# Loading v of four more blocks as fp16 on GpSimd's queue, and turning q and k of four more blocks by DMA, in a fused sliding-window attention and MLP kernel

## The chip, the cores and the metric

The kernel runs on one core of one Trainium2 chip. The metric is the device time of one execution in microseconds. Before the change the median of 8 runs is 321.86 us (321.04 to 322.49).

## What is computed

q, k and v are fp32 tensors of 8 batches, 8 heads, 576 positions and 64 values per head. Attention looks back over a window of 128 positions and carries a bias that falls with distance. Its output, 4608 rows of 512, goes through a layer norm with a gain and a two-layer MLP with a residual. Cut to what matters:

```
scores = scale * q @ k.T
scores = where((rel >= 0) & (rel < 128), scores - slope_h * abs(rel), -1e9)
x  = softmax(scores) @ v                     # all heads side by side: 4608 x 512
xn = (x - mean) / sqrt(var + 1e-6) * g_ln
out = x + relu(xn @ w_ch1) @ w_ch2           # 512 x 2048 and 2048 x 512
```

## The kernel before, in words

The 4608 rows are cut into 36 blocks of 128. One pair of batches has nine blocks (`PERIOD`), and the fifth of these holds the end of one batch and the start of the next, so its loads come in two halves.

**Attention, block by block** (`attention(i)`, L527). q and k are loaded, made fp16, and turned so that the head dimension lies on the partitions (`qkt`). The scores of a block against itself and the block before it go to PSUM (L687), with the bias added by a matmul with a distance table in blocks 0 to 4 (L703) and multiplied in afterwards as a mask table from block 5 on (L742). ScalarE takes the exponential (L735). TensorE multiplies with `vx`, v in fp16 with a column of ones (L759), and VectorE divides (L776, L780), takes the statistics (L797, L802) and makes `xs` (L808). `xs` is turned into `xt`, by TensorE for blocks 0 to 11 (L820) and by DMA from 12 on (L835).

**MLP, chunk by chunk** (`mlp(c)`, L857). Blocks are gathered in chunks of 3, 2, 3 and then 4. For each of 16 slices of the hidden layer four matmuls (L869) go to a PSUM bank, and ScalarE or VectorE takes the ReLU (L881, L879). Then, for each block, four groups of four matmuls (L897) follow, VectorE adds the residual (L905), and SP stores the block (L913). Below, a *weight group* is four such matmuls. The weights are loaded as fp16 by GpSimd's queue in eight pieces of 512 KB (L518, L520), four of each matrix.

**How q, k and v come in.** There are three ways.
- *Spans* (`SPANS`, L453): blocks 0 and 1, 2 and 3, 5 and 6, 7 and 8 load q and k of two blocks in one 512 KB DMA on SP's queue. An engine casts it (L594, L596), TensorE turns it in 4 fp32 transposes (L603).
- *Plain loads* (L358): q and k of block 4, and v of blocks 0 to 8, come as fp32 on SP's queue, and GpSimd or ScalarE casts them (L540, L542, L573, L575).
- *Cast loads* (`load_cast`, L461 and L466): from block 9 on (`LOAD_CAST`), q, k and v come as fp16 by a casting DMA on GpSimd's queue.

The fp16 q and k of blocks 4 and 9 to 12 are turned by TensorE in 8 transposes (L649) and evicted from PSUM (L657, L659); from block 13 on (`QK_BY_DMA`) they are turned by a DMA on SP's queue (L664).

**What sets the order.** All work is given to a planner (`Plan`, L47) as tasks with costs, dependencies, priorities and due times. It plays the queues and engines through and writes down the order in which every engine's instructions stand; each engine then runs its own list in that order. The tables `PICK` (which engines may take a cast or an eviction), `PRI`, `HOLD` and `SLACK` steer it. `LANDING` holds the latencies that it assumes for DMAs. `TABLE_AFTER` and `MIX_AFTER` name the block after whose product with v the mask tables may be made (L431, L439). Up to block `SPLIT` the scores are made in two halves. Up to 26 us of planned time (`WARM`), planned gaps of TensorE are filled with warm-up matmuls (L932).

`W_AFTER` says behind which step each weight piece is issued: a third of the number is a block, the rest says q, k or v of it. All cast loads wait for the last piece:

```
W_AFTER = [9, 10, 11, 12, 20, 23, 26, 28]
t_w[n] = plan.transfer(f"w{n}", "POOL", 0.8, 3.2, 0.0, emit, [casts[at % 3]] + last, av(i, -60.0))
for t in cast_loads:
    t.deps.append(t_w[7][0])
```

In a span, each of the three stands for the cast of v. So the first three pieces follow the cast of v of block 3.

Of the kernel before, what the change touches and what calls it, by code (L numbers as in the profile page):

```python
# [10 lines left out]
FP16 = mybir.dt.float16  # L11
# [35 lines left out]
class Plan:  # L47
# [8 lines left out]
    LANDING = {"DMA SP": (0.7, 1.3), "DMA ACT": (0.7, 1.3), "DMA POOL": (1.6, 1.4)}  # L56
# [170 lines left out]
def kernel(  # L227
# [15 lines left out]
    P = 128  # L243
# [26 lines left out]
    TABLE_AFTER = 2  # L270
    MIX_AFTER = 3
    SPLIT = 4
    LOAD_CAST = 9
    HALVED = []
    SPANS = [0, 2, 5, 7]
    SLACK = (0.1, 0.2, 0)
    PICK = {('xt', 0): 'ACT DVE', ('xt', 8): 'ACT', ('cv', 5): 'POOL', ('cv', 0): 'ACT', ('ev', 8): 'DVE', ('ev', 1): 'DVE', ('ev', 3): 'ACT', ('ck', 8): 'ACT', ('cq', 5): 'POOL', ('ev', 5): 'ACT', ('ck', 2): 'POOL', ('ck', 7): 'ACT', ('cq', 6): 'POOL', ('cq', 2): 'ACT', ('xt', 6): 'ACT DVE', ('cq', 8): 'POOL', ('xt', 5): 'DVE', ('cv', 7): 'POOL ACT', ('cv', 3): 'POOL', ('xt', 3): 'DVE', ('ev00', 4): 'DVE ACT', ('cs1', 1): 'POOL', ('cs0', 0): 'POOL', ('ev10', 3): 'ACT', ('xt', 2): 'ACT DVE', ('cq', 3): 'POOL', ('cs0', 8): 'POOL', ('ev01', 8): 'DVE ACT', ('ev10', 8): 'DVE ACT', ('ev11', 5): 'ACT', ('cs0', 2): 'ACT', ('cq', 4): 'POOL ACT', ('ev00', 8): 'DVE ACT', ('ev01', 0): 'DVE', ('cv', 8): 'POOL', ('ev11', 0): 'ACT', ('cv', 4): 'POOL ACT', ('ev01', 6): 'DVE', ('cv', 6): 'ACT', ('ev10', 5): 'ACT', ('cs1', 4): 'POOL ACT', ('ev', 0): 'DVE ACT', ('cv', 2): 'POOL', ('ev00', 2): 'DVE ACT', ('ev00', 7): 'ACT', ('ev10', 2): 'ACT', ('xt', 1): 'ACT', ('ev11', 8): 'ACT', ('xt', 4): 'DVE', ('ev00', 1): 'DVE', ('cv', 1): 'ACT', ('ev01', 7): 'DVE ACT', ('ev11', 6): 'DVE ACT', ('cq', 1): 'POOL ACT', ('ev01', 4): 'DVE ACT', ('cs0', 5): 'ACT', ('ev', 7): 'DVE ACT', ('xt', 7): 'ACT', ('ev', 9): 'ACT', ('cv', 9): 'POOL', ('cq', 11): 'POOL', ('cs1', 9): 'POOL ACT', ('ev00', 10): 'ACT', ('eva', 5): 'DVE', ('cka', 9): 'POOL DVE ACT', ('cv', 11): 'ACT', ('cqa', 10): 'POOL', ('ckb', 10): 'POOL', ('ck', 10): 'ACT', ('ev00', 5): 'DVE ACT', ('ckb', 3): 'POOL ACT', ('evb', 5): 'DVE ACT', ('ev', 11): 'DVE ACT', ('ev01', 2): 'DVE ACT', ('ckb', 6): 'ACT', ('eva', 11): 'ACT', ('cqb', 7): 'POOL', ('cka', 1): 'ACT', ('ev00', 3): 'DVE ACT', ('cq', 0): 'POOL', ('ev01', 5): 'ACT', ('cqb', 5): 'DVE', ('ev10', 4): 'DVE ACT', ('ev01', 9): 'DVE', ('cqa', 8): 'POOL DVE ACT', ('ev10', 10): 'DVE ACT', ('evb', 4): 'ACT', ('cqb', 8): 'POOL DVE ACT', ('cs0', 9): 'POOL', ('cka', 3): 'DVE', ('cqa', 2): 'DVE', ('cka', 8): 'ACT', ('cqa', 5): 'DVE', ('cq', 7): 'ACT', ('ck', 1): 'POOL ACT', ('cka', 0): 'ACT', ('cqa', 7): 'POOL', ('ev10', 11): 'ACT', ('cqa', 4): 'POOL DVE ACT', ('ev11', 11): 'ACT', ('eva', 10): 'ACT', ('ev11', 4): 'DVE', ('eva', 3): 'ACT', ('ev11', 2): 'DVE ACT', ('cqa', 6): 'DVE', ('cqa', 9): 'DVE', ('cqa', 11): 'POOL', ('ev', 2): 'DVE ACT', ('cs0', 4): 'POOL DVE', ('ckb', 11): 'POOL ACT', ('ckb', 2): 'POOL', ('ck', 5): 'POOL', ('cs1', 8): 'ACT', ('ev01', 10): 'DVE ACT', ('ev', 10): 'ACT', ('cq', 10): 'ACT', ('eva', 4): 'DVE ACT', ('cv', 10): 'ACT', ('ev', 6): 'DVE ACT', ('ck', 11): 'ACT', ('cs1', 11): 'POOL ACT', ('cqb', 1): 'DVE', ('ckb', 7): 'DVE', ('ev11', 1): 'ACT', ('ck', 4): 'ACT', ('cka', 11): 'DVE', ('ckb', 0): 'ACT', ('cs1', 0): 'POOL DVE', ('eva', 7): 'DVE ACT', ('cs0', 11): 'POOL ACT', ('evb', 8): 'DVE ACT', ('ev10', 6): 'DVE', ('eva', 2): 'DVE', ('cqb', 2): 'POOL DVE ACT', ('cq', 9): 'POOL ACT', ('ev10', 9): 'DVE', ('ev10', 0): 'DVE', ('evb', 6): 'DVE', ('eva', 8): 'ACT', ('cqa', 3): 'DVE', ('ck', 9): 'POOL ACT', ('evb', 3): 'DVE', ('cs0', 1): 'POOL', ('cqb', 9): 'ACT', ('cqb', 0): 'DVE', ('evb', 2): 'DVE ACT', ('evb', 1): 'DVE ACT', ('cqb', 6): 'ACT', ('eva', 9): 'DVE ACT', ('evb', 10): 'ACT', ('cqb', 11): 'DVE', ('cka', 10): 'POOL ACT', ('ck', 6): 'POOL', ('ckb', 1): 'POOL', ('ev10', 7): 'DVE ACT', ('cs1', 7): 'POOL', ('ev01', 3): 'DVE ACT', ('cs0', 7): 'POOL', ('cs0', 6): 'POOL ACT', ('cs1', 3): 'ACT', ('cka', 2): 'POOL', ('cqa', 1): 'ACT', ('ev01', 1): 'DVE ACT', ('cs0', 10): 'POOL ACT', ('cka', 4): 'POOL ACT', ('ev00', 6): 'ACT', ('xt', 10): 'ACT DVE'}
    PRI = {'mnewc': 2.9, 'Sa2': 1.9, 'nm0.4': 4.0, 'eT5.01': 6.2, 'pva1': -8.8, 'exb1': -4.1, 'xt0': -3.9, 'r0.14': -4.9, 'ks7.i': 6.9}
    HOLD = {'w5.i': 45.07, 'T7.1': 46.04, 'exb6': 45.43, 'r1.2': 36.4, 'eT2.01': 14.22, 'bn7': 65.04, 'r0.5': 30.1, 'bn0': 12.95, 'v1.i': 2.75, 'r1.4': 36.86, 'rc0.3': 22.89, 'rs1': 31.48}
    BY_BIAS = 5  # L280
    MASK_AT = 5
    QK_BY_DMA = 13
# [8 lines left out]
    def ring(name, n, shape, dt):  # L291
        return plan.ring([sb(f"{name}{i}", shape, dt) for i in range(n)])
# [16 lines left out]
    v32 = ring("v32", 5, [P, H, D], FP32)  # L309
    qk16 = ring("qk16", 6, [P, 2, d_model], FP16)  # L310
    vx = ring("vx", 7, [P, H, VD], FP16)
# [94 lines left out]
    d_row = plan.transfer("g", "ACT", 0.5, 0.02, 0.0, lambda e, b: nc.scalar.dma_start(out=g_row[:, :], in_=moe_g_ln.unsqueeze(0)), (), -8e5)[1]  # L406
# [42 lines left out]
    def load_span(name, src, r, n, i, v):  # L449
        (_, _, b, s0), = where(i)  # L450

        def emit(e, bank):
            nc.sync.dma_start(  # L453
                out=r[n][:, :, :],
                in_=src[b, :, s0 : s0 + 2 * P, :].rearrange("h (p t) d -> p h (t d)", t=2),
            )
        t, d = plan.transfer(f"{name}{i}", "SP", 0.6, 1.75, 1.0, emit, (), v)
        r.writes(n, t)
        return d

    def load_cast(name, src, i, dst, v):  # L461

        got = []
        for p0, n, b, s0 in where(i):
            def emit(e, bank, p0=p0, n=n, b=b, s0=s0):
                nc.gpsimd.dma_start(out=dst(p0, n), in_=src[b, :, s0 : s0 + n, :].rearrange("h p d -> p h d"))  # L466
            got.append(plan.transfer(f"{name}{i}", "POOL", 1.0 if n == P else 0.9, 1.24 if n == P else 0.76, 0.0, emit, (), v))
        return [t for t, d in got], [d for t, d in got]

# [3 lines left out]
    cast_loads = []  # L473
    for i in range(NBLK):
        nrm[i] = len([1 for j in range(i) if j not in span_of])
    for i in range(NBLK):
        vl = av(i) - 300
        if i in span_of:
            n = span_of[i]
            if SPANS[n] == i:  # L480
                span_load[n] = (load_span("qs", q, qs, n, i, vl), load_span("ks", k, ks, n, i, vl + 0.01))
            loads[i] = (None, None, load("v", v, v32, i, vl + 0.02))
            continue
        if i in HALVED:
            part = [slice(0, H // 2), slice(H // 2, H)]
            qk = [[load("qk"[a] + "ab"[x], (q, k)[a], (q32, k32)[a], i, vl + 0.004 * x + 0.002 * a, nrm[i], part[x]) for x in range(2)] for a in range(2)]
            loads[i] = (qk[0], qk[1], load("v", v, v32, i, vl + 0.02))
            continue
        if i >= LOAD_CAST:
            m = nrm[i]  # L490
            tq, dq_ = load_cast("q", q, i, lambda p0, n, m=m: qk16[m][p0 : p0 + n, 0, :].rearrange("p (h d) -> p h d", d=D), vl)
            tk, dk_ = load_cast("k", k, i, lambda p0, n, m=m: qk16[m][p0 : p0 + n, 1, :].rearrange("p (h d) -> p h d", d=D), vl + 0.01)
            tv, dv_ = load_cast("v", v, i, lambda p0, n, i=i: vx[i][p0 : p0 + n, :, 0:D], vl + 0.02)
            cast_loads += tq + tk + tv
            for t in tq + tk:
                qk16.writes(m, t)
            for t in tv:
                vx.writes(i, t)
            loads[i] = (dq_, dk_, dv_)
            continue  # L500
        loads[i] = (
            load("q", q, q32, i, vl, nrm[i]),
            load("k", k, k32, i, vl + 0.01, nrm[i]),
            load("v", v, v32, i, vl + 0.02),
        )

    W_AFTER = [9, 10, 11, 12, 20, 23, 26, 28]
# [19 lines left out]
    def attention(i):  # L527
# [48 lines left out]
        if i < LOAD_CAST:  # L576
            cv = [add(f"cv{i}", pick("cv", "POOL", POOL=0.64, ACT=0.62), e_cv, lv_, av(i, 0.2))]
            v32.reads(i, cv[0]); vx.writes(i, cv[0])
            weights(i, (cv[0],) * 3 if i in span_of else (cq[-1], ck[-1], cv[0]))
        else:  # L580
            weights(i, (None, None, None))
# [341 lines left out]
    for t in cast_loads:  # L923
        t.deps.append(t_w[7][0])
# [48 lines left out]
```

## Time and profile before

| what | before |
|---|---|
| median of 8 runs | 321.86 us |
| the profiled execution's own time | 322.49 us |
| its span, first to last instruction | 320.8 us |
| TensorE busy | 313.2 us (98%) |
| VectorE, ScalarE, GpSimd busy | 182.8, 166.1, 95.0 us |
| transposes of fp16 q and k on TensorE (L649) | 40 |
| warm-up matmuls (L932) | 102 |
| DMA transposes of q and k (L664), time to landing | 23, 3.0 to 9.1 us |
| granted TensorE clock | 1.00 |

How to read the page: PE is the matmul row of TensorE, PEld its weight loads, DVE is VectorE, ACT ScalarE, POOL GpSimd, SP the sync engine that issues DMAs. Times are in microseconds from the first instruction. In a timeline a line gives start, duration, engine, source line, operation, output<-inputs and the number of instructions; in brackets stands the idle time before it and what ended it. The slices show the busy tenths in 40 equal parts of the span. In the table of stretches each line has the stretch, its length, and then busy time and number of instructions of PE, PEld, DVE, ACT and POOL, the clock, the busy share of the DMA engines and GB/s. A matmul's shown duration is longer than the distance to the next one, since they are pipelined; costs are therefore read from start to start.

### The profile page before, as it was taken

What the parts mean: (1) busy time and instruction counts of PE and PEld (TensorE: products, weight loads), DVE (VectorE), ACT (ScalarE), POOL (GpSimd) and SP (SyncE); (2) the same over time, 40 slices, a digit from 0 to 9 for tenths busy, and PEclk for the clock granted to TensorE, in tenths of its full rate; (3) what the DMA queues carried; (4) which work ended last, traced back from release to release, by engine and by line L of the source; (5) the groups of instructions that cost most, each with busy time, mean ns of one, the idle gap of its engine ahead of it and who ended that gap; (6) DMA issues with size and microseconds to landing.
All of it is one profiled execution on the core that took longest, in us unless ns stands there. A gap on an engine that the chain in (4) does not pass through costs nothing.

```text
span 320.8 us, 6445 instructions
## 1 busy us (share of the span) xinstructions
PE 313.2 (98%) x2584; PEld 170.9 (53%) x2584; DVE 182.8 (57%) x408; ACT 166.1 (52%) x269; POOL 95.0 (30%) x124
## 2 busy tenths in 40 slices
PE   8998999999999999999999999999999999999995
PEld 6875675466645554444454445444444454444453
DVE  3597387299745856755665566546655665221012
ACT  2987885059705852475257525752575257305600
POOL 4250349468631816803372531201100000000000
PEclk9999999999999999999999999999999999999999
DMA  8999988999999999999999999727700220011011
GB/s 192 233 203 211 222 160 123 172 230 166 155 142 199 140 108 112 172 173 143 173 170 177 86 165 182 80 51 131 133 16 18 82 85 16 19 66 65 2 65 65
DMA packets 151120, 40.93 MB, mean 128 GB/s; under 512 B 134065, under 2 KB 146609, under 8 KB 151090
## 3 DMA queue, kind: packets, MB, share of 16 engines
q0 software_dynamic: 88608, 14.82, 64.6%
q1 hardware_dynamic: 62480, 25.70, 38.5%
q8 instruction: 20, 0.33, 0.4%
q14 instruction: 10, 0.08, 0.1%
q10 hardware_dynamic: 2, 0.00, 0.0%
HBM read 36.70 MB, written 9.44 MB: 144 GB/s over the span
## 4 chain that ended last, share of the span: by engine, by line
PE 87%; DMA 5%; DVE 3%; SPq 3%; issue 0%; POOL 0%
PE fb L897 39%; PE fb L869 37%; PE sc L687 5%; PE fb L759 4%; DMA w1sb<-in_moe_w_ch_dram 3%; DMA v<-in_v_dram 2%; SPq L358 1%; SPq L453 1%; DVE xs L808 1%; PE fb L820 1%; PE fb L649 1%; PE fb L603 1%; DVE ot L905 0%; DVE st L797 0%; DVE xb L780 0%
## 5 line engine op out<-in xcount | busy, mean ns | idle before, releaser
L869 PE MATMUL fb<-xt,w1sb 128*128 128x512 f16 (+2 forms) x640 | 133.6, 358 | 1.5 <-DMA w1sb<-in_moe_w_ch_dram 1.4
L897 PE MATMUL fb<-w2sb,ht 128*128 128x512 f16 (+1 forms) x592 | 134.2, 373 | 0.0
L881 ACT ACTIVATE ht<-fb 128x512 f16<-128x512 f32 (+2 forms) x144 | 80.4, 562 | 81.0 <-PE fb L869 79.2
L869 PEld LDWEIGHTS <-w1sb 128*128 128x128 f16 x640 | 59.9, 98 | 56.9 <-DMA w1sb<-in_moe_w_ch_dram 1.9
L735 ACT ACTIVATE probs<-sc 128x1024 f16<-128x1024 f32 (+1 forms) x72 | 67.2, 974 | 35.5 <-PE sc L687 35.5
L897 PEld LDWEIGHTS <-ht 128*128 128x128 f16 x592 | 54.7, 98 | 57.8
L905 DVE SCALAR_TENSOR_TENSOR ot<-fb,rstd,xb 128x512 f32<-128x512 f32 (+1 forms) x37 | 27.3, 737 | 62.6 <-PE fb L897 62.0
L466 POOL DMA_DIRECT2D vx<-in_v_dram x30 | 25.4, 847 | 92.1 <-PE fb L759 89.0
L742 DVE TENSOR_TENSOR probs<-probs,mreg 128x1024 f16<-128x1024 f16 (+1 forms) x48 | 30.5, 653 | 23.1 <-ACT probs L735 22.8
L780 DVE TENSOR_TENSOR xb<-fb,rec 128x256 f16<-128x256 f32 x72 | 30.2, 422 | 2.1
L759 PEld LDWEIGHTS <-probs 128*128 128x128 f16 x544 | 24.7, 97 | 11.4
L808 DVE SCALAR_TENSOR_TENSOR xs<-xb,mv,g_t 128x512 f16<-128x512 f16 x36 | 28.4, 790 | 1.0
L466 POOL DMA_DIRECT2D qk<-in_q_dram x30 | 25.9, 867 | 5.8 <-DMA w2sb<-in_moe_w_ch_dram 2.6
L759 PE MATMUL fb<-vx,probs 128*128 128x65 f16 x544 | 26.9, 193 | 0.0
L466 POOL DMA_DIRECT2D qk<-in_k_dram x30 | 26.0, 873 | 2.2 <-DMA w2sb<-in_moe_w_ch_dram 1.7
L797 DVE BATCH_NORM_STATS2 st<-xb 128x6 f32<-128x512 f16 x36 | 24.9, 693 | 1.0
L776 DVE RECIPROCAL rec<-fb 128x4 f32<-128x4 f32 x72 | 12.5, 177 | 19.0 <-PE fb L759 18.9
L687 PEld LDWEIGHTS <-qkt 64*128 64x128 f16 x544 | 15.3, 94 | 11.9 <-issue 11.1
L687 PE MATMUL sc<-qkt 64*128 64x128 f16 x288 | 19.4, 216 | 0.0
L687 PE MATMUL sc<-qkt,qkt 64*128 64x128 f16 x256 | 18.2, 219 | 0.0
L879 DVE TENSOR_SCALAR ht<-fb 128x256 f16<-128x256 f32 (+2 forms) x16 | 8.7, 548 | 8.1 <-PE fb L869 7.6
L596 POOL CAST ks<-ks 128x1024 f16<-128x1024 f32 x3 | 4.0, 1331 | 22.1 <-DMA ks<-in_k_dram 22.1
(61 smaller groups left out, 122.4 us busy)
## 6 DMA issues: line engine op xcount, KB each, us to landing
out_dram<-ot SPq DMA_DIRECT2D x35, 256.0 KB, 2.8
qk<-in_q_dram POOLq DMA_DIRECT2D x24, 128.0 KB, 7.2
qk<-in_k_dram POOLq DMA_DIRECT2D x24, 128.0 KB, 7.2
vx<-in_v_dram POOLq DMA_DIRECT2D x24, 128.0 KB, 5.2
qs<-in_q_dram SPq DMA_DIRECT2D x4, 512.0 KB, 7.9
ks<-in_k_dram SPq DMA_DIRECT2D x4, 512.0 KB, 7.6
v<-in_v_dram SPq DMA_DIRECT2D x8, 256.0 KB, 6.3
w1sb<-in_moe_w_ch_dram POOLq DMA_DIRECT2D x4, 512.0 KB, 11.2
```

The costliest lines, as they stand in the source:

```text
L466: nc.gpsimd.dma_start(out=dst(p0, n), in_=src[b, :, s0 : s0 + n, :].rearrange("h p d -> p h d"))
L687: nc.tensor.matmul(scs[half][:, g, c0 : c0 + P], kt[rows, 1, hp, :], qkt[i][rows, 0, hp, :], start=not bias, stop=True, skip_group_check=True,
L735: nc.scalar.activation(out=o, in_=n_, func=AF.Exp, scale=inv_sqrt_d)
L742: en.tensor_tensor(out=pv, in0=pv, in1=mask[:, 2 * half : 2 * half + 2, :, lo:], op=ALU.mult)
L759: nc.tensor.matmul(pp[:, hh * (D + 1) : hh * (D + 1) + D + 1], probs[i][:, bank, slot, side * P : side * P + P], vx[i - 1 + side][:, h, 0 ...
L780: nc.vector.tensor_tensor(out=xb[i][:, 256 * half : 256 * half + 256].rearrange("p (h d) -> p h d", d=D), in0=pp[:, :, 0:D], in1=rec[2 * i ...
L797: nc.vector.bn_stats(out=st[i][:, :], in_=xb[i][:, :])
L808: nc.vector.scalar_tensor_tensor(out=xs[i][:, :], in0=xb[i][:, :], scalar=mv[c][:, j, 0:1], in1=g_t[:, :], op0=ALU.subtract, op1=ALU.mult,)
L869: nc.tensor.matmul(fb[b][:, 0:n_], w1sb[:, kb, f * P : f * P + P], xt[c][:, kb, 0:n_], start=(kb == 0), stop=(kb == NKB - 1),)
L881: nc.scalar.activation(out=ht[c][:, f, 0:n_], in_=src, func=AF.Relu)
L897: nc.tensor.matmul(pm[:, 0 : c1 - c0], ht[c][:, f, j * P : j * P + P], w2sb[:, f, c0:c1], start=(f == 0), stop=(f == NFB - 1),)
L905: nc.vector.scalar_tensor_tensor(out=ot[i][:, c0:c1], in0=fb[plan.held[key][1]][:, 0 : c1 - c0], scalar=rstd[c][:, j : j + 1], in1=xb[i][: ...
```

## The change

v of blocks 5 to 8 (`V_CAST`) is loaded by the casting DMA straight into `vx`, so that the fp32 loads and casts of these four blocks go. `W_AFTER` changes: the first weight piece follows the cast of v of block 2, the next two that of block 3, the fourth the load of v of block 5, the fifth and sixth that of block 7, the last two the load of k of block 9. The cast loads no longer wait for the last weight piece; they are chained in order of block, each behind the load before it and the pieces that stand ahead of it. `QK_BY_DMA` falls from 13 to 8; as 7 and 8 are a span, q and k of blocks 9 to 12 are now turned by DMA. The mask tables are allowed one block later, block 4's scores are made in two halves, some costs that the planner assumes change, and `PICK`, `PRI`, `HOLD` and `SLACK` are new.

The instructions counted in both programs: plain v loads on SP fall from 10 to 6, cast loads of v on GpSimd rise from 30 to 34, casts of v fall from 9 to 5, transposes of fp16 q and k on TensorE from 40 to 8, their 128x1024 evictions from 5 to 1, DMA transposes of q and k rise from 23 to 27, warm-up matmuls fall from 102 to 97. On SP's queue v of block 1 now stands ahead of q of blocks 2 and 3. GpSimd's list of DMAs begins: weight piece 0, 1, 2, v of 5, piece 3, v of 6, v of 7, pieces 4 and 5, the cast of q of 7 and 8, v of 8, q and k of 9, the cast of k of 7 and 8, pieces 6 and 7. Between pieces 0 and 1 stand the casts of v of 3 and q of 4, between pieces 2 and v of 5 the cast of v of 4. On TensorE the first half of block 4's product with v now stands ahead of the first MLP matmul, and the q turn of blocks 5 and 6 stands eight weight groups after that point instead of six.

```diff
-    LANDING = {"DMA SP": (0.7, 1.3), "DMA ACT": (0.7, 1.3), "DMA POOL": (1.6, 1.4)}
+    LANDING = {"DMA SP": (0.7, 1.3), "DMA ACT": (0.7, 1.3), "DMA POOL": (2.1, 1.4)}
...
-    TABLE_AFTER = 2
-    MIX_AFTER = 3
-    SPLIT = 4
+    TABLE_AFTER = 3
+    MIX_AFTER = 4
+    SPLIT = 5
     LOAD_CAST = 9
+    V_CAST = 5
...
-    SLACK = (0.1, 0.2, 0)
+    SLACK = (0, 0.3, 0)
...
-    QK_BY_DMA = 13
+    QK_BY_DMA = 8
...
+    def load_v(i, v):
+        if i < V_CAST:
+            return load("v", v_in, v32, i, v)
+        tv, dv_ = load_cast("v", v_in, i, lambda p0, n: vx[i][p0 : p0 + n, :, 0:D], v)
+        cast_seq.append((3 * i + 2, tv))
+        for t in tv:
+            vx.writes(i, t)
+        return dv_
...
-    W_AFTER = [9, 10, 11, 12, 20, 23, 26, 28]
+    W_AFTER = [7, 10, 10, 17, 22, 22, 28, 28]
...
+        seq = dict(cast_seq)
+        third = seq[3 * i + 2][-1] if i >= V_CAST else cv[0]
+        if i in span_of:
+            weights(i, (third,) * 3)
+        elif i >= LOAD_CAST:
+            weights(i, (seq[3 * i][-1], seq[3 * i + 1][-1], third))
+        else:
+            weights(i, (cq[-1], ck[-1], third))
...
-    for t in cast_loads:
-        t.deps.append(t_w[7][0])
+    cast_seq.sort(key=lambda x: x[0])
+    for n, (at, tasks) in enumerate(cast_seq):
+        before = [t_w[m][0] for m, w_at in enumerate(W_AFTER) if (w_at // 3 * 3 + 2 if w_at // 3 in span_of else w_at) < at][-1:] + (cast_seq[n - 1][1] if n and at < 27 else [])
+        for t in tasks:
+            t.deps += before
```

## The prediction

> **What bounds the kernel now.** I read the page's busy row and slices first, then the busy time by stretches, then the first 45 us of TensorE and GpSimd in order of time, then the chain that ended last, and at the end the DMA issues.
>
> The page says where the limit is:
>
> ```profile
> PE 313.2 (98%) x2584; PEld 170.9 (53%) x2584; DVE 182.8 (57%) x408; ACT 166.1 (52%) x269; POOL 95.0 (30%) x124
> PE   8998999999999999999999999999999999999995
> PEclk9999999999999999999999999999999999999999
> ```
>
> TensorE is the bound and its clock is full throughout, so only work taken off it, or waits and fillers, can move the end. By stretches:
>
> ```profile
> 20.00:26.00 6.00, 4.24 (x77) 3.50 (x76) 4.98 (x14) 6.00 (x14) 2.03 (x3) 1.00 1.16 213
> 42.00:50.00 8.00, 7.56 (x96) 6.32 (x94) 7.55 (x18) 5.79 (x12) 4.13 (x6) 1.00 0.65 113
> 90.00:120.00 30.00, 30.00 (x240) 14.96 (x239) 18.28 (x38) 16.41 (x25) 11.51 (x14) 1.00 1.71 151
> ```
>
> The second figure is TensorE. From 90 us it never idles. What can be won or lost is the work itself and the first 90 us: 1.76 us idle at 20 to 26, 0.44 at 42 to 50, and the warm-up matmuls that fill the rest before 26. TensorE in order of time:
>
> ```profile
> 20.37 0.62 PE L649 MATMUL fb<-iden,qk 128*128 128x128 f16 x8
> 20.82 0.41 PE L759 MATMUL fb<-vx,probs 128*128 128x65 f16 x8
> ...
> 24.07 0.45 PE L932 MATMUL fb<-warm_t 128*128 128x128 f16 x5
> 25.93 1.47 PE L869 MATMUL fb<-xt,w1sb 128*128 128x384 f16 x8 [1.41 <-DMA w1sb<-in_moe_w_ch_dram]
> 27.24 0.41 PE L759 MATMUL fb<-vx,probs 128*128 128x65 f16 x8
> ...
> 30.88 0.60 PE L603 MATMUL fb<-iden,qs 128*128 128x128 f32 x4
> ```
>
> The first MLP matmul waits 1.41 us for the first weight piece. The chain says why that piece is late, and GpSimd's row shows the order in which it is issued:
>
> ```profile
> 9.68 7.25 DMA v<-in_v_dram
> 16.93 0.05 issue
> 16.98 0.56 POOL vx L575
> 17.54 8.35 DMA w1sb<-in_moe_w_ch_dram
> ```
> ```profile
> 14.32 0.62 POOL L575 CAST vx<-v 128x512 f16<-128x512 f32 x1
> 16.98 0.62 POOL L575 CAST vx<-v 128x512 f16<-128x512 f32 x1 [2.05 <-DMA v<-in_v_dram]
> 17.54 0.92 POOL L518 DMA_DIRECT2D w1sb<-in_moe_w_ch_dram  x1
> ```
>
> The piece is issued behind the cast of v of block 3, whose load lands at 16.93, and lands at 25.89.
>
> **Transposes of blocks 9 to 12 (QK_BY_DMA).** Only four blocks move, since 7 and 8 are a span. Each loses 8 transposes; in the rows above the next instruction starts 0.45 us after them (20.37 to 20.82), as at 68.03, 72.86 and 81.94. 4 x 0.45 = **-1.8 us**, straight off the bound. Four evictions of 128x1024 go too (0.67 us on VectorE, 1.02 on ScalarE), off the path. Four DMA transposes come onto SP's queue, between stores; the 23 existing ones land 3.0 to 9.1 us after issue. In the new order the q and k of block 9 are issued ahead of the last two weight pieces, and its scores stand 20 us of TensorE work after the first use of the second matrix, those of 10 to 12 later still, so I take 0. If that cover were gone, each late block would cost at most its 9.1 us less the weight work queued ahead of it.
>
> **First weight piece.** W_AFTER puts it behind the cast of v of block 2, which ran at 14.32 to 14.88, so it is issued at 14.88: 2.66 earlier. The same 8.35 makes it land at 23.2. That piece alone would free the start: the last turn of chunk 0 (xt, VectorE at 23.62 for 0.42) ends at 24.04, so the first MLP matmul could run at 24.1 and not 25.93, **-1.8**. The instruction counts fit: 97 warm-up matmuls for 102.
>
> **What the earlier piece collides with.** Packets of the two queues, counted from the trace (KB per us):
>
> ```
> 17.5-19.0  SP alone, 256-byte packets    about 190
> 19.5-20.5  SP alone, 512-byte packets    about 240
> 21.5-28    GpSimd's 1 KB packets 140, SP's 512-byte packets  72
> 31-34      GpSimd's 1 KB packets 146, SP's 256-byte packets  36
> ```
>
> GpSimd's first packet left at 20.37, 2.83 us after its issue, when the 256-byte loads up to v of block 4 had finished (19.3). Moved by 2.66 it leaves at 17.7 and is near full flow at 18.3, with some 170 KB of v of block 4 outstanding: 170/36 = 4.7 us, so 23.1 instead of 19.3. A completion took 1.1 us (data at 19.3, landing at 20.39): landing 24.2, cast 0.6, and its first product with the probabilities, which in the new order stands *ahead of* the first MLP matmul, is at 24.8 and takes 0.25. First MLP matmul about 25.1, 0.8 earlier than now.
>
> The next is q of blocks 5 and 6 (512 KB, landed 26.83 before). It now starts at 23.1: 512/72 = 7.1, plus 1.1, lands at 31.3; ScalarE's cast takes 1.36, so its turn on TensorE can run at 32.7 and not 30.88. TensorE gets there at 25.1 + 8 weight groups x 0.667 + 0.55 = 31.0 and waits 1.7 us. It has done two groups more than before by then (1.33), so it is 32.7 - 30.88 - 1.33 = **+0.5 us behind**, the 0.8 spent. k of the same span then lands by 38.4 (7.1 later), is cast by 40, and is wanted at 32.7 + 7.7 = 40.4: 0.
>
> A rule of the Trainium skill would make this worse: DMA: Bandwidth & Descriptors, under Specifications, gives GpSimd's path a first byte after about 1 us. With it the packets would start at 15.9, with most of k and v of block 4 (over 400 KB) still to come: 11 us at 36 KB/us, and the first MLP matmul near 29. The row says 2.83 (and 2.7 at the second weight matrix); I take the row.
>
> **v of blocks 5 to 8.** Four 256 KB fp32 loads and their four casts (GpSimd 0.61, 1.05, 0.62; ScalarE 0.63) go; four 128 KB cast loads come, each 0.9 us of GpSimd. The same page and section says that rows under 512 bytes fall below line rate, against halving v's rows to 128 bytes. In the trace cast loads queued without company land 0.95 us apart (61.69, 62.67, 63.61, 64.55), an fp32 load 1.29 after the one before it (12.97, 14.26). By the rule each would be dearer than what it replaces, some 2 us in all before the second matrix; by the row cheaper. I take the row: 0, and the casts were off the path. What they do is clear SP's queue: the second q/k span no longer stands behind v of block 5 (landing 38.61).
>
> **Second weight matrix, and what waits on GpSimd.** Its first two pieces no longer sit behind casts (issued 38.31 and 47.82 before); they follow the queue of 512 KB at 3.65 us each and land some 4 us earlier. But the last two stand behind GpSimd's casts of q and k of blocks 7 and 8, so a late span delays them and the cast loads between. Cost between -0.4 (the 0.41 us that TensorE waits near 48 for VectorE's xs of block 5 vanishes) and +2.5 (below); the nearest row is that 0.41, met by an order that is no longer there: -0.4.
>
> **Masks, split of block 4, picks.** Mask tables move behind block 4's first exponentials (8 x 0.3 us on ScalarE, which is full at 20 to 26), which lets the product of block 4 stand ahead of the first MLP matmul. If they delay the first ReLUs: three PSUM banks give about 2 us of cover; beyond it up to 0.5. I take 0. The new engine choices move evictions between engines at 52 and 57%: 0, bounds -0.3 and +0.3.
>
> **Sum.** -1.8 + 0.5 - 0.4 = -1.7 on the profiled 322.49 (span 320.80 and 1.69 around it), giving 320.8. That execution is 0.63 above the median of 321.86; on the median 320.2.
>
> **Rivals.**
> *No collision.* SP's loads keep pace (loads of one queue overlap, so less is outstanding than I count). Then -1.8 (turns), -1.8 (start), -0.25 (product already done), -0.4: **317.6**. For it: the first idle is 1.41 us and goes in full. Against: the 36 KB/us row.
> *Slower: SP starved behind GpSimd.* The place is the q of blocks 7 and 8. If q of 5 and 6 needs another 0.8 us, and three spans flow at 72 KB/us without relief, q of 7 lands at 32.1 + 2 x 7.1 = 46.3 at worst, about 45 with part of the queue empty; cast 1.33 on GpSimd: the turn runs at 46.4 for 43.38 now, with 0.2 us more done: +2.8, and the last weight pieces follow. -1.8 + 2.8 = +1.0, less part of 0.4: **322.6**. It decides when the loss before 50 us passes 2.2. Against: the small v packets between weights leave SP more.
> *The turns give nothing.* A DMA transpose of 9 to 12 is late, or TensorE waits as long as it saved: **321.8**.
>
> **How the numbers follow.** Forecast 0.40 (319.0 to 321.3), no collision 0.25 (317.2 to 318.8), starved 0.23 (322.4 to 323.5), nothing 0.12. A measurement of this kernel tells about 0.2%, 0.64 us, from no change. Faster 0.60 (forecast nearly whole, no collision), same 0.16, slower 0.24. The range takes the forecast, most of no collision and the nearer half of starved: 317.5 to 322.9.
>
> **What would show it.** Right: 8 instead of 40 transposes of qk on TensorE; the first piece issued near 14.9 and landed near 23.2; the first MLP matmul at 25.1, released by v of block 4; a wait of 1 to 2 us at the q turn of blocks 5 and 6 near 32.7; no idle after 90. Wrong: that turn before 31 (no collision), or idle over 1 us at the turns of 7 or at the last pieces of the second matrix (starved); a first piece that still lands at 25 would break the step that everything in the start rests on.

## The result and the profile after

The changed kernel takes 319.69 us in the median of 12 executions (319.01 to 321.83), the kernel before 321.98 (33 executions on the same chip, 321.04 to 325.42 and one of 462.0); the ratio is 0.9932 with a 95% interval of 0.9914 to 0.9949. The profiled executions stand at 320.42 (span 318.7) and 322.49 (span 320.8): 2.07 us. Executions of one kernel differ by some us (by 2.8 for the changed kernel), in part through a collision that the experiments bring out, so a run's range is given with its median.

The busy row of the page after:

```profile
PE 311.3 (98%) x2547; PEld 169.2 (53%) x2547; DVE 180.7 (57%) x411; ACT 164.3 (52%) x261; POOL 96.9 (30%) x125
```

TensorE is still the bound, with 1.9 us less to do. The stretches (after the length: TensorE, its weight loads, VectorE, ScalarE, GpSimd, then clock, DMA share, GB/s):

```profile
20.00:26.00 6.00, 6.00 (x100) 4.80 (x98) 5.71 (x17) 5.43 (x10) 3.30 (x4) 1.00 1.21 237
26.00:34.00 8.00, 7.34 (x56) 4.59 (x55) 6.48 (x16) 7.16 (x18) 3.00 (x4) 1.00 1.30 216
34.00:42.00 8.00, 6.65 (x51) 4.79 (x50) 1.87 (x5) 5.16 (x10) 4.83 (x5) 1.00 1.45 204
42.00:50.00 8.00, 8.00 (x104) 6.15 (x102) 6.69 (x17) 5.41 (x8) 5.79 (x8) 1.00 1.62 191
```

The idle time at 20 to 26 and at 42 to 50 is gone; a new one of 1.35 us stands at 34 to 42, and 0.66 at 26 to 34 (0.18 before). TensorE in order of time shows where:

```profile
24.61 0.42 PE L773 MATMUL fb<-vx,probs 128*128 128x65 f16 x8
24.86 1.46 PE L883 MATMUL fb<-xt,w1sb 128*128 128x384 f16 x8
...
28.70 2.77 PE L883 MATMUL fb<-xt,w1sb 128*128 128x384 f16 x16 [0.29 <-DVE mnew L440]
31.31 0.60 PE L617 MATMUL fb<-iden,qs 128*128 128x128 f32 x4
31.75 0.39 PE L834 MATMUL fb<-iden,xs 128*128 128x128 f16 x4
32.43 5.39 PE L883 MATMUL fb<-xt,w1sb 128*128 128x384 f16 x40 [0.29 <-DMA w1sb<-in_moe_w_ch_dram]
39.17 1.47 PE L883 MATMUL fb<-xt,w1sb 128*128 128x384 f16 x8 [1.35 <-DMA w1sb<-in_moe_w_ch_dram]
```

The first MLP matmul runs at 24.86 (25.93 before) and waits for nothing; the q turn of blocks 5 and 6 (L617) waits for nothing either. The longest wait is now for the fourth weight piece. The chain that ended last, and GpSimd in order of time, say the same:

```profile
24.64 14.48 DMA w1sb<-in_moe_w_ch_dram
39.12 0.05 issue
39.17 1.47 PE fb L883 x8
```
```profile
14.27 1.05 POOL L582 CAST vx<-v 128x512 f16<-128x512 f32 x1
15.27 0.92 POOL L525 DMA_DIRECT2D w1sb<-in_moe_w_ch_dram  x1
...
17.94 0.62 POOL L549 CAST qk<-q 128x512 f16<-128x512 f32 x1 [1.13 <-DMA q<-in_q_dram]
18.50 1.48 POOL L525 DMA_DIRECT2D w1sb<-in_moe_w_ch_dram  x2
...
23.76 0.89 POOL L467 DMA_DIRECT2D vx<-in_v_dram  x1
24.64 0.76 POOL L525 DMA_DIRECT2D w1sb<-in_moe_w_ch_dram  x1
```

The first piece is issued at 15.27 and lands at 21.52. The fourth stands behind v of block 5: issued at 24.64, landed at 39.12.

### The profile page after: what moved, and what is told of

It reads as the page before. It is cut to its first block, busy times and chain, and to the rows that moved or that the text cites. A ratio compares the mean times of both kernels' runs of the same rounds, so it can differ in the third digit from the quotient of the medians.

```text
span 318.7 us, 6377 instructions
## 1 busy us (share of the span) xinstructions
PE 311.3 (98%) x2547; PEld 169.2 (53%) x2547; DVE 180.7 (57%) x411; ACT 164.3 (52%) x261; POOL 96.9 (30%) x125
## 4 chain that ended last, share of the span: by engine, by line
PE 92%; DMA 5%; DVE 1%; ACT 1%; issue 0%
PE fb L911 40%; PE fb L883 36%; PE sc L701 6%; PE fb L773 5%; DMA w1sb<-in_moe_w_ch_dram 5%; PE fb L949 2%; PE sc L717 1%; PE fb L617 1%; PE fb L834 1%; PE fb L410 1%; ACT probs L749 0%; DVE xb L794 0%; DVE xs L822 0%; DVE st L811 0%; ACT qkt L627 0%
## 5 line engine op out<-in xcount | busy, mean ns | idle before, releaser
L911 PE MATMUL fb<-w2sb,ht 128*128 128x512 f16 (+1 forms) x592 | 135.8, 373 | 0.0
L467 POOL DMA_DIRECT2D vx<-in_v_dram x34 | 28.8, 847 | 67.3 <-PE fb L773 54.6
L467 POOL DMA_DIRECT2D qk<-in_k_dram x30 | 25.3, 845 | 14.6 <-DMA vx<-in_v_dram 8.1
L773 PE MATMUL fb<-vx,probs 128*128 128x65 f16 x544 | 27.5, 193 | 0.2 <-ACT probs L749 0.2
L822 DVE SCALAR_TENSOR_TENSOR xs<-xb,mv,g_t 128x512 f16<-128x512 f16 x36 | 27.0, 750 | 0.9
L893 DVE TENSOR_SCALAR ht<-fb 128x256 f16<-128x256 f32 (+2 forms) x19 | 9.8, 524 | 14.2 <-PE fb L883 13.9
L949 PE MATMUL fb<-warm_t 128*128 128x128 f16 x97 | 9.5, 257 | 1.1 <-DVE warm_t L371 1.1
## 6 DMA issues: line engine op xcount, KB each, us to landing
qk<-in_q_dram POOLq DMA_DIRECT2D x24, 128.0 KB, 10.4
ks<-in_k_dram SPq DMA_DIRECT2D x4, 512.0 KB, 10.4
```

The lines of the kernel that those rows point to most:

```text
L773: nc.tensor.matmul(pp[:, hh * (D + 1) : hh * (D + 1) + D + 1], probs[i][:, bank, slot, side * P : side * P + P], vx[i - 1 + side][:, h, 0 ...
L822: nc.vector.scalar_tensor_tensor(out=xs[i][:, :], in0=xb[i][:, :], scalar=mv[c][:, j, 0:1], in1=g_t[:, :], op0=ALU.subtract, op1=ALU.mult,)
L911: nc.tensor.matmul(pm[:, 0 : c1 - c0], ht[c][:, f, j * P : j * P + P], w2sb[:, f, c0:c1], start=(f == 0), stop=(f == NFB - 1),)
```

## The experiments

Twelve kernels, each timed beside the kernel before on the same chip. e5, e9, e10 and e7 ran on another chip than the rest. The kernel before has medians of 321.80 to 322.12 in these rounds, so a difference of some 0.3 us between kernels of different rounds says nothing. No run takes back v's cast loads, the later mask tables or the split of block 4 alone.

**1. Parts taken back, and the planner run anew.** In these, one number is changed (in e4 two) and the planner orders all engines again.

```diff
e1_turns_back:        QK_BY_DMA = 8 -> 13
e2_turns_alone:       (kernel before) QK_BY_DMA = 13 -> 8
e3_w3_before_v5:      W_AFTER = [7, 10, 10, 17, ...] -> [7, 10, 10, 14, ...]
e4_w3_with_w2:        W_AFTER -> [7, 10, 10, 10, ...], and one hold for the cast of v of block 4
```

> The changed kernel with q and k of blocks 9 to 12 turned by TensorE again (32 matmuls more, 40 in all). My theory, that these turns are bound time and nothing waits for their DMA: 1.9 us slower than the changed kernel, about 321.6 against 319.7. Rival, that TensorE waits elsewhere for as long as it saved, so that the gain comes from the start and the new order: no more than 0.6 us slower, about 320.

Measured: 322.81 (321.38 to 325.12), ratio 1.0022 [1.0001, 1.0043]. That is 1.2 more than I expected; a part of the reason stands below e4.

> The kernel before with only the turns of blocks 9 to 12 moved to DMA; loads, pieces and tables as before. My theory: 1.9 us faster than before, about 320.0, which is nearly the whole change. Rival, that the turns pay only with v's new loads and the new order: within 0.6 us of before. In this kernel q and k of block 9 come behind the last weight piece (landing near 62), so the turn by DMA can make block 9's scores late: up to 1 us of the gain may go there.

Measured: 334.73, ratio 1.0403 [1.0371, 1.0434]. It is 14.7 us above my expectation, and the rival (no change) missed it too. The turned q and k of block 10 land at 77.1, but its scores stand at 91.6 with no wait in front: the new order puts the scores of blocks 10 to 13 between 91.6 and 100.7, where TensorE then waits for VectorE (1.9 us for masked probabilities, 1.4 for `xs`) and its granted clock falls. The stretch of e2:

```profile
90.00:105.00 15.00, 11.51 (x146) 6.96 (x145) 12.23 (x29) 9.26 (x12) 4.38 (x5) 0.77 2.15 183
```

> The changed kernel with the fourth weight piece ahead of the load of v of block 5 on GpSimd's queue. The changed kernel waited 1.35 us for this piece (landing 39.12). My theory, that v's small packets ahead of it and its late issue make it late: it lands near 36, that wait goes, and the time falls by 1.0 to 1.4, about 318.5. Rival, that the queues' total is the limit and the wait only moves to what comes behind (v of 5, k of 5 and 6, q of 7 and 8): within 0.5 of 319.7.

Measured: 319.33 (318.99 to 322.52), ratio 0.9935 [0.991, 0.996]; the 1.35 us wait is gone and the profiled span is 317.7 for 318.7. By the medians only 0.36 is gained, the rival's "within 0.5": the new plan has a wait of its own, on VectorE.

```profile
54.59 0.38 PE L834 MATMUL fb<-iden,xs 128*128 128x128 f16 x4 [0.41 <-DVE xb L794]
```

> The changed kernel with the fourth weight piece right behind the third, ahead of the cast of v of block 4 as well (that cast goes to ScalarE), so that GpSimd's wait of 2.7 us for v of block 4 no longer holds it up. My theory: the piece lands near 35, its wait goes, 318.4 or a little more, since the third run already removes it. Rival, that the early weight traffic starves q and k of blocks 5 and 6: waits of 1 to 2 us at their turns, 319.7 or slower.

Measured: 321.63 (319.28 to 323.82), ratio 0.9973 [0.9941, 1.0005]. The time is the rival's, but the wait isn't (it had q and k of blocks 5 and 6). Five executions stand at 319.3 to 320.7, seven at 321.6 to 323.8.

What e1 and e4 have in common is in their profiles at the turn of block 4, which the changed kernel's profile passes without a wait. TensorE in order of time in e1, then its stretches:

```profile
22.74 0.40 PE L663 MATMUL fb<-iden,qk 128*128 128x128 f16 x4 [2.57 <-ACT qk L547]
```
```profile
20.00:26.00 6.00, 2.92 (x42) 2.02 (x38) 2.70 (x7) 3.44 (x6) 1.66 (x2) 0.90 1.23 236
26.00:34.00 8.00, 7.93 (x77) 5.39 (x76) 6.56 (x18) 6.74 (x14) 4.89 (x7) 0.86 1.30 216
```

ScalarE's cast of k waits for its load, which lands at 21.97 in e1 and 21.82 in e4, against 18.59 in the changed kernel and 19.62 in e3. In e1 and e4 SP issues the second half of that k at 15.62 and 14.99, in the other two at 13.96 and 13.97. GpSimd's first packets leave at 16.7 to 17.2 in all four, and from 18 to 20 us SP moves only 1 to 30 KB per us. TensorE waits 2.6 to 2.7 us, and the granted clock is 0.90 and 0.86 in the two stretches, because part of the work there runs at half rate: warm-up matmuls near 27.5 start 107 ns apart again, in place of 56. So a collision of the kind that I forecast exists, at another load, and in some executions only.

**2. Does a later first piece end it?** The first piece behind the cast of v of block 3 again, with the planner run anew.

```diff
e5_first_piece_back:        W_AFTER = [7, 10, 10, 17, ...] -> [9, 10, 10, 17, ...]
e9_first_back_w3_early:     W_AFTER = [7, 10, 10, 17, ...] -> [9, 10, 10, 14, ...]
e10_first_back_turns_back:  as e9, and QK_BY_DMA = 8 -> 13
e7_old_tables:              SLACK, PICK, PRI, HOLD -> those of the kernel before
```

> The first weight piece goes behind GpSimd's cast of v of block 3 again (its place in the queue before the change), all else as in the changed kernel. Theory (a race of the first piece with k of block 4: the changed kernel takes 319.0 to 319.7 where k has landed by 19.6 and about 322 where it lands at 21.9): the cast waits for v of block 3 to land at 15.4 to 17.2, so the piece is issued at 16.5 to 17.8 and its packets begin no earlier than 18.3; k has landed by 19 in every execution, no wait at the turn of block 4, first MLP product at 24.9 to 25.5, 319.3 to 320.0, and no execution above 320.7. Rival (the early piece is itself what the change gains; the race is no more than chance): the first MLP product goes back to 26, about 320.8. Second rival (the 2.6 us wait at the turn of block 4 has another cause than the weight piece): slow executions stay, 319 to 322.

Measured: 323.32 (322.95 to 323.98), ratio 1.0033 [1.002, 1.0046]. k of block 4 landed at 19.00 and its turn did not wait, as expected; the time was 3.3 us above the top of what I expected. The profile has the stall that the prediction gave to the change itself, and later ones:

```profile
29.77 0.65 PE L617 MATMUL fb<-iden,qs 128*128 128x128 f32 x4 [1.32 <-ACT qs L608]
33.91 2.77 PE L883 MATMUL fb<-xt,w1sb 128*128 128x384 f16 x16 [0.66 <-DMA w1sb<-in_moe_w_ch_dram]
40.08 2.12 PE L883 MATMUL fb<-xt,w1sb 128*128 128x384 f16 x12 [1.10 <-DMA w1sb<-in_moe_w_ch_dram]
```

q of blocks 5 and 6 lands at 28.30 here, at 25.50 in the changed kernel. The planner also issues the third piece only at 23.87 (19.23 in the changed kernel), so not all of the loss is the first piece's.

> The two moves together: the first weight piece behind the cast of v of block 3, and the fourth piece ahead of v of block 5 (which took away the 1.35 us wait at 37.6). Theory: neither wait is left; 318.5 to 319.1, no execution above 320, and so faster than the changed kernel by 0.5 to 1. Rival (the late first piece costs the TensorE 0.5 to 1 us at 25): 319.5 to 320.

Measured: 322.97 (321.96 to 323.6), ratio 1.0009 [0.9985, 1.0034]: wrong by 4 us, with 1.66 us of TensorE's idle time between 42 and 60 alone, where the changed kernel has none.

> The kernel with both moves, and q and k of blocks 9 to 12 turned by TensorE again: what the turns by DMA are worth where no weight piece disturbs k of block 4. Theory (the prediction's step: four turns at 0.45 us): 1.8 us above the kernel with both moves, 320.3 to 320.9, with q and k turns again at 2.3 us of TensorE's pitch in place of 0.46. Rival (with v landing earlier, TensorE waits at these turns in any case, and what is taken off comes back as waits): within 0.4 us of the kernel with both moves. Second rival (the loss of 3.1 us seen with the turns back in the changed kernel was all turns and not a wait at block 4): 321.7 or more.

Measured: 324.13 (323.65 to 325.29), ratio 1.0066 [1.005, 1.0081]: 1.16 above e9 by the medians, 1.7 by the profiled spans (321.9 and 320.2), near the first theory in the difference; the level is not, since e9 itself came out 4 us high.

> The changed kernel with the planner's tables of before (slack, engine picks, priorities, holds): what the new order is worth by itself. Theory (turns by DMA under the old tables lost 12.8 us through an order that puts the attention of blocks 10 to 12 in one stretch, so that the order must be made for the turns): slower than the changed kernel by 3 to 12 us, with TensorE waits for probs between 90 and 150 and a granted clock below 0.95 there. Rival (that order came from v and the weight pieces being late, not from the tables): within 1 us of the changed kernel, 319 to 321.

Measured: 323.01 (322.03 to 328.27), ratio 1.0042 [1.0013, 1.0071]: 3.3 us above the changed kernel, the low end of the theory, but without its waits for probs: the clock is 1.00 and TensorE full from 60 us on, and 2.26 us are idle between 50 and 60.

These runs have a fault in common: each new plan moved hundreds of instructions, so a part and its order could not be told apart.

**3. One pair of instructions at a time, all else in the same order.** The planner's list is taken as it is and edited afterwards.

```diff
 e11_same_order_first_late
     order = plan.run()
+    names = [t.name for t, e, b in order]
+    first = order.pop(names.index("w0.i"))
+    order.insert(names.index("cv3"), first)
 e13_same_order_w3_first
     order = plan.run()
+    names = [t.name for t, e, b in order]
+    first = next(n for n, x in enumerate(names) if x == "v5.i")
+    order.insert(first, order.pop(names.index("w3.i")))
 e12_same_order_turns_pe  (cut; QT9 to QT12 leave the list; where a PSUM bank opens next:)
+                    for a in range(2):
+                        for hp in range(HP):
+                            nc.tensor.transpose(pt[:, a, hp, :], qk16[nrm[i]][:, a, hp * P : hp * P + P], iden[:, :])
 e14_before_order_turns_dma  (kernel before; in T9 to T12, and ev9 to ev12 empty)
+                    nc.sync.dma_start_transpose(
+                        out=qkt[i][:, :, :, :].rearrange("p a hp c -> p (a hp) c"),
+                        in_=qk16[nrm[i]][:, :, :].rearrange("p a d -> p (a d)"),
+                    )
```

> The changed kernel with the order of every engine left as it is, but for one pair on GpSimd: the issue of the first weight piece stands behind the cast of v of block 3 in place of ahead of it. (The earlier run with the piece back was planned anew, so that all else moved too.) Theory (a race of the piece with k of block 4, and 3 us to spare at the first MLP product): the piece is issued near 16.2 to 16.9 and lands near 23, the first MLP product stays at 24.9 to 25.0, k of block 4 lands by 19 in every execution; 319.0 to 320.0, none above 320.7. Rival (issued later, the piece meets the packets of q of blocks 5 and 6, as in the run planned anew, where these landed at 28.3 and TensorE waited 1.3 us for them): 320.5 to 321.5, with a wait of about 1.3 us at the turn near 31. Second rival (the loss of 3.6 us in the run planned anew came from the piece and not from the new plan): 322 to 323.5.

Measured: 320.77 (320.16 to 322.27), ratio 0.9968 [0.995, 0.9985]. About 1.1 above the changed kernel by the medians: the size is the first rival's, but not its wait. In the profile q of 5 and 6 does land late, at 29.11, but its turn runs at 31.86 without a wait. The first MLP matmul stands at 25.44 for 24.86, and TensorE's clock happened to rise later here (after 10.4 us for 9.1), before the moved piece can matter. So how the later piece costs 1.1 us is not shown by this profile.

> The changed kernel with its order left as it is, but with q and k of blocks 9 to 12 turned by TensorE (8 products each, at the first point behind the old issue where a PSUM bank opens) and taken out of PSUM by VectorE, in place of the turn by DMA. Theory (the prediction's step, 4 times 0.45 us, and the measured pitch of 2.36 against 0.46 us): 1.8 to 1.9 above the changed kernel, 321.1 to 321.7, with no new wait. Rival (the turns lie in stretches where TensorE waits anyway, and the gain came from the new order): within 0.4 of the changed kernel. Second rival (the turned q and k by VectorE come late, or hold up what is behind them): 322 or more.

Measured: 324.74 (324.24 to 325.46), ratio 1.0079 [1.0058, 1.0101]. The level is the second rival's: something is held up behind the turns. TensorE in order of time, at the first of the four turns:

```profile
54.73 0.61 PE L683 MATMUL fb<-iden,qk 128*128 128x128 f16 x8
56.11 0.38 PE L843 MATMUL fb<-iden,xs 128*128 128x128 f16 x4 [0.78 <-DVE qkt L684]
```

From the first product's start to the next instruction's the four turns take 5.57 us: 32 x 56 ns = 1.79 of work, and four times 0.94 because the next product in my list needs the bank that VectorE has yet to empty. That second part is my placement, not the turns. Without it (324.74 - 3.78, an estimate) 320.96 is left, 1.3 above the changed kernel.

Up to 54 us TensorE's list is that of the changed kernel, so this profile is also a second execution of it. The wait for the fourth piece, 1.35 us in the other, is shorter here, since the pieces ahead of it landed 1.5 us earlier:

```profile
37.92 1.47 PE L892 MATMUL fb<-xt,w1sb 128*128 128x384 f16 x8 [0.32 <-DMA w1sb<-in_moe_w_ch_dram]
```

> The changed kernel with its order left as it is, but for one pair on GpSimd: the fourth weight piece is issued ahead of v of block 5 in place of behind it. Theory (the 1.35 us wait at 37.6 is for the fourth piece, which lies behind the 3 us that the small packets of v of block 5 took): the piece lands at 36 to 36.5, the wait goes, v of block 5 lands at 39 and nobody waits for it; 1.0 to 1.35 below the changed kernel, 318.2 to 318.8. Rival (v of block 5, 3.5 us later, is then what comes last, as the run planned anew showed no more than 0.4 to 1.0 of gain): 319.2 to 319.7, with a new wait between 39 and 55.

Measured: 319.11 (318.5 to 324.2), ratio 0.9916 [0.9892, 0.9941], the lowest of all. In the stretches TensorE is full where the changed kernel waited 1.35 us:

```profile
34.00:42.00 8.00, 8.00 (x73) 5.88 (x72) 2.19 (x5) 6.38 (x13) 3.22 (x4) 1.00 1.54 204
```

The piece landed at 35.78, v of block 5 at 38.83, and no wait of TensorE ends on it. By the medians 0.58 is gained, and the two intervals overlap. That is less than the theory's 1.0 to 1.35 and more than the rival's, and the rival's new wait is there, though VectorE ends it and not v:

```profile
44.91 0.40 PE L773 MATMUL fb<-vx,probs 128*128 128x65 f16 x8 [0.52 <-DVE ht L893]
```

> The kernel of before with its order left as it is, but q and k of blocks 9 to 12 turned by SP's queue, at the place where TensorE turned them, and no copy out of PSUM. (The earlier run with these turns alone was planned anew and lost 12.8 us to an order with the attention of blocks 10 to 12 in one stretch.) Theory (the turns pay only where q and k of blocks 9 to 12 come earlier, which the early weight pieces bring about: here q and k of block 9 land at 61.7 and 62.7, and a turn by DMA takes 8 us to land, while the scores of block 9 stand at 69.4): TensorE saves 1.9 us and waits 1.5 to 6 us for turned q and k at 69 to 90; 322 to 326. Rival (the 8 us are hidden): 320.0 to 320.4. Second rival (turns by DMA hold up SP's queue and GpSimd's loads beside them, as in the run planned anew): 327 or more.

Measured: 336.53, ratio 1.0439 [1.0411, 1.0467], in the second rival's range and not in mine. TensorE in order of time:

```profile
74.69 0.61 PE L695 MATMUL sc<-qkt 64*128 64x128 f16 x8 [5.61 <-DMA qkt<-qk]
89.31 0.29 PE L695 MATMUL sc<-qkt,qkt 64*128 64x128 f16 x2 [6.76 <-DMA qkt<-qk]
```

Two waits, 12.4 us, and a granted clock of 0.73 at 75 to 90. The first is the turn's own latency: issued at 65.81, landed at 74.64. The second is its queue: q and k of block 11 had landed by 67.5, but on SP their turn stands behind an output store that is issued at 80.07, and goes out at 80.58.

**The collision, counted.** Executions without a profile show only their mean granted clock. I take 0.995 or less as the mark of the collision, since the profiles of e1 and e4 have 0.994 and 0.995; no marked execution of another kernel has a profile, and the kernel before has the mark too in 3 of 74, by what cause is not known. It can also count too few: e13's profile, with k landed at 20.71 and waits of 1.23 and 0.52 us, has 0.999. With the first piece ahead of the cast of v of block 3 (the changed kernel, e1, e3, e4, e7, e12, e13) these are 20 of 77 (1 of 12 in the changed kernel, 6 of 12 in e4), with it behind (e5, e9, e10, e11) none of 35. The mark does not explain all of e1's excess: its eight executions without it have a median of 322.55, still 0.9 above what I expected.

## Why the prediction came out right, and where its steps did not

**The turns of blocks 9 to 12: -1.8, right.** From start to start the products for fp16 q and k fall from 2.36 us in all to 0.46, by 1.9. The runs put it at 1.2 to 1.8 (e10 against e9; e12 less its own waits). The cover that I named, that the scores of block 9 stand long behind the landing, is what carries it: turned q and k of block 9 land at 58.2 and are used at 67.0. In the kernel before, where TensorE turned them at 66.6, the same turns by DMA lose 14.7 us (e14). So they don't pay by themselves; the earlier loads of q and k of block 9 (landed by 49.75, by 62.67 before) belong to the edit as much. The price of the lost cover was too low: I had at most 9.1 us less the queued work for each, and left out that a turn can stand behind a store on SP.

**The first piece and the start: right in effect, its packets not.** Forecast: issued 14.88, landed 23.2, first MLP matmul at 25.1. Measured: 15.27, 21.52, 24.86, so -1.07 in place of -0.8, and the product of block 4 (0.25) already done, as forecast. The first packet left 1.63 us after the issue, not 2.83, and the 1.63 lies between my row and the 1 us of the Trainium skill (DMA: Bandwidth & Descriptors, Specifications); the start at 29 that I worked out from the latter did not come. The start differs between executions too: e12's, in the same order, has it at 25.64. With the order kept, e11 puts the early piece at 1.1 us by the medians, collision included.

**The collision at q of 5 and 6: +0.5 behind, wrong.** This step failed. I let v of block 4 land at 24.2 and q at 31.3 and made TensorE wait 1.7 us; they landed at 22.57 and 25.50 and it waited for neither. The packets, counted from the traces in KB per us by the end of each, show why:

```
             changed kernel                e11 (piece behind the cast)
        GpSimd 1 KB  SP 256 B  SP 512 B    GpSimd 1 KB  SP 256 B  SP 512 B
17-18        42         19         0             1        133         0
18-19       196          3         0            48         18         0
19-20       169         24         0           123         26         0
20-21       104        122         0           154         39         0
21-22         1        110       149           141         44        10
22-23         0          0       268            44         14       244
23-24       121          0        90            69          1       192
```

The two queues do share as I said, SP at 3 to 24 KB per us beside the piece (18 to 20 us). But I let GpSimd's stream run on from the first piece to the second. It didn't: the second is issued at 18.50, behind the cast of q of block 4, its first packets leave 4.4 us later, and in the hole from 21 to 22.9 SP moves nearly all of q of 5 and 6. By 23.5, when the second stream is under way, 503 KB have moved in 512-byte packets, nearly q's 512 (the packets don't say whose they are). In e5, where the first piece came later, 436 had moved by 24; q landed at 28.3 and TensorE waited 1.32. A later piece does not always do this: in e9 and e10 q landed at 26.28 and 25.48, and TensorE waited 0.47 and 0.33. The mechanism was right, its place was not: with the early piece it strikes k of block 4, in the profiles of e1, e4 and e13, and costs some 2.8 us between e4's two groups.

**v of blocks 5 to 8: 0, wrong by the 1.35 us of the new wait.** I weighed the rule against rows under 512 bytes and took the row of 0.95 us for a cast load. That row had been measured without company. Here v of block 5 landed 3.09 us after the piece before it (35.47 after 32.38), beside SP's 512-byte packets: 39 to 40 KB per us in 128-byte packets against their 161 to 163 (31 to 33 us). The fourth piece, behind it, landed at 39.12. The rule's estimate, about 2 us in all, was the nearer. e13 shows that v's place ahead of the piece is the cause of this wait: with the piece first the wait is gone. Its size belongs to the execution (0.32 in e12's), and by the medians e13 gains 0.58, not 1.35.

**What else waited: -0.4, wrong on the whole.** The 0.41 us near 48 vanished, as forecast, but two new waits of 0.29 stand at 28.7 and 32.4: +0.17 together. The first ends with VectorE's copy of a mask table (L440), which I had put at 0 with a bound of 0.5; the second is for the third weight piece.

**The sum.** Forecast -1.7 on the profiled execution: -1.8, +0.5, -0.4. Measured: -1.9 (turns), -1.32 (start, with the product done), +1.35 (fourth piece), +0.58 (the two small waits), -0.41: -1.70, of the 2.07 seen. The other 0.37 I did not follow. The total agrees by luck in this part: a stall of about the forecast's size came 7 us later than forecast, for another piece. With the order kept, e11 and e12 put the early piece at 1.1 and the turns at 1.3 to 1.8, together about the 2.3 of the medians. The rival without a collision (317.6) describes the start well and misses that wait; the starved one did not come, q of 7 and 8 was turned at 44.19 without a wait.

**The order.** I gave the new tables 0 (-0.3 to +0.3). e7 puts them at 3.3 us, yet that can't be called their worth: e1, e5, e9 and e7 had a new order made by tables not fitted to them, and each lost 3.1 us or more by the medians, more than the whole gain (e3 and e4, planned anew too, did not). What the order is worth by itself stays open. So does why SP issues the second half of k of block 4 at 14 in some executions and at 14.9 to 15.6 in others (15.41 in the kernel before, where no piece is on its way yet), and where the later piece of e11 costs its 1.1 us.

## What to carry to other kernels

Where a planner orders the work, undoing a part and planning anew measures the new plan; to price one edit, keep the recorded order and move one pair of instructions. A transfer's rate from a row holds only beside the company it had there: ask which packets will share the engines, of what size, and whether the other queue has a hole. Work moved from the bound engine to a DMA queue is free only if its data are early by the landing time and nothing that waits stands ahead of it in that queue.

## What the runs showed of the hardware that I had not expected

TensorE starts at half rate, and when it rises differs between executions by over 6 us. The small fp32 matmul of the gain row (L410), in the changed kernel and then in e13:

```profile
4.06 2.07 PE L410 MATMUL fb<-ot,ot 1*128 1x512 f32 x2
6.07 1.67 PE L949 MATMUL fb<-warm_t 128*128 128x128 f16 x14
```
```profile
3.92 1.12 PE L410 MATMUL fb<-ot,ot 1*128 1x512 f32 x2
4.98 0.95 PE L952 MATMUL fb<-warm_t 128*128 128x128 f16 x14
```

Warm-up matmuls start 107 ns apart and later 56. The change comes between 2.9 and 5.0 us in e13, after 9.03 in the changed kernel, between 11.2 and 12.0 in e3, though the first matmul runs at 1.07 in all three; the profile's clock column says 1.00 in these first us all the while. The Trainium skill, TensorE: Matmul & The Clock Gate, Part 1, has the rise some 4 us into sustained work, within 0.5 us; these traces spread wider, from under 3.9 us behind the first matmul (e13) to over 10 (e3). An early rise puts the first q turn 1.1 us ahead (6.45 for 7.53). The three profiles with a late k of block 4 (e1, e4, e13) are the three with the earliest rise, which may be chance or may be what decides; no run here tells.

In e1 waits of 2.57 and 0.52 us, in a stretch where TensorE was busy for 2.92 of 6 us, were followed by 3.4 us at half the clock, so they cost more than their length:

```profile
24.80:28.20 3.40, 3.40 (x38) 2.54 (x37) 2.52 (x7) 2.74 (x6) 3.15 (x4) 0.50 1.20 214
```

In e13 waits of 1.23 and 0.52 us, with 4.25 of the same 6 us busy, left it at 1.00.
